# A weight decoder's sign words: read from the scaled word in SBUF instead of the raw word, in a fused attention and two-layer expert kernel

## The chip, the cores and the metric

The kernel runs on one core of a Trainium2 chip. The metric is device microseconds of one execution, lower is better; the time of a kernel is the median of its runs.

## The reference

Windowed attention with four sink positions is followed by two expert layers, each on the output of the one before. The inputs are float32 values that were multiplied by 8 and come to the kernel as float64.

```python
# attention: 2 batches, 8 heads, 768 positions, head size 64
scores = np.where(is_sink | in_window, scale * q @ k.T, -1e9)   # window 128, 4 sinks
a = exp(scores - max); a = a / (a.sum() + 1e-9); x = a @ v      # -> (1536, 512)
# first layer, 512 -> 2048 -> 512
h = np.maximum(x @ w_in, 0.0)
x = h * h @ w_out
# second layer, 512 -> 2048 -> 512
h = x @ w_in
P = a[0] + a[1] * h + a[2] * h**2 + a[3] * h**3
Q = 1.0 + abs(b[0]) * abs(h) + abs(b[1]) * h**2
return (P / (Q + 1e-6)) @ w_out
```

## The kernel before

**Weights.** Each layer's hidden size of 2048 is cut into 16 chunks of 128. A chunk holds the 512 x 128 piece of `w_in` and the 128 x 512 piece of `w_out` as 128 partitions x 1024 columns, so there are 32 chunks. `load_chunk` brings one in as two halves of 512 columns, here called a pair of halves; there are 64 halves. Each half comes by one DMA of 512 KB (L56, queue of SP) as two 32-bit words for each weight, the low and the high word of the float64, into a raw tile `wr` (three buffers). ScalarE scales the high word as if it were a float32 (L63, into `wt`), and writes the sign of the high word as a 16-bit value into the upper half of each word of a sign tile (L65; two sign tiles are used in turn). VectorE shifts the low word and puts the sign into it (L66, in place in `wr`), then shifts `wt` and puts that in (L67, in place in `wt`). The float32 weight stands in `wt` then; ScalarE casts it to the matmul type (L299, tile `wh`) and GpSimd takes the rest (L300, tile `wl`). `wt` has two buffers, and one comes free with L300 of its half. The raw tile comes free with its last reader, L67.

**Matmuls.** Every product is made of three: high x high, low x high, high x low. A unit is one chunk on one group of tokens: `gemm1` makes h (L400, 12 matmuls), an activation follows, its result is split into gh and gl (L407 ScalarE, L409 GpSimd), and `gemm2` adds to four accumulators (L439 in the first layer, L441 in the second, 12 matmuls). A unit of 512 tokens is 24 matmuls. The activation of the first layer is a relu (L128, ScalarE) and a product (L130, VectorE); that of the second is a rational function: L159, L161, L163, L168, L169 on ScalarE, L164 on GpSimd, L165, L166, L170, L171, L172 on VectorE.

**Stages.** Each layer works through its chunks in three stages of 6, 5 and 5. In a stage, all groups of tokens pass its chunks; then the accumulators are added to a sum in SBUF by VectorE (L465 in the later stages). The first stage of the first layer has six groups of 256 tokens and runs among the attention's blocks, each named by batch, pair of 256 positions and pair of heads, as e_1_2; the later stages have three groups of 512. Seven slots (`WSLOTS`) hold chunks, and four more are there from the second stage on, when the attention's pools are closed. A chunk is loaded into the slot of one whose last group has passed.

**Order.** The work is written in the order of the units, and a scheduler that knows the operations' dependencies turns it into a fixed order for each engine. An instruction waits for its semaphores, and all behind it on its engine wait too. The four L465 of a group stand in VectorE's order among the L66 and L67 of halves that are loaded meanwhile, and the first matmuls of the next group's accumulators can't start until these L465 have read the old ones. In the attention, the row maxima and masked scores come from VectorE (L341), and matmuls of the scores (L329) need the buffers that these free.

Of the kernel before, what the change touches and what calls it, by code (L numbers as in the profile page):

```python
# [10 lines left out]
F16 = mybir.dt.float16  # L11
# [29 lines left out]
def f32(ap):  # L41
    return ap.bitcast(F32)
# [10 lines left out]
def narrowed(nc, pool, src, n, signs):  # L53

    raw = pool.tile([P, 512, 2], U32, tag="wr", name=f"wr{n}", bufs=3)
    nc.sync.dma_start(raw.rearrange("p c w -> p (c w)"), src.bitcast(U32))  # L56
    lo, hi = raw[:, :, 0], raw[:, :, 1]
    t = pool.tile([P, 512], U32, tag="wt", name=f"wt{n}")
    s = signs[0]
    signs.append(signs.pop(0))  # L60


    nc.scalar.mul(f32(t), f32(hi), 2.0**-112)  # L63

    nc.scalar.mul(s.bitcast(F16).rearrange("p (c w) -> p c w", w=2)[:, :, 1], f32(hi), 2.0**-112)  # L65
    nc.vector.scalar_tensor_tensor(out=lo, in0=lo, scalar=29, in1=s, op0=ALU.logical_shift_right, op1=ALU.bitwise_or)  # L66
    nc.vector.scalar_tensor_tensor(out=t, in0=t, scalar=3, in1=lo, op0=ALU.logical_shift_left, op1=ALU.bitwise_or)  # L67
    return f32(t)
# [107 lines left out]
def banded(ctx, tc, const, qk0, qk1, vb, vs, ns_f, win_f, wp, ab, scalars, out):  # L176
# [115 lines left out]
    def load_chunk(L, pool=wpool):  # L292
        home[L] = pool
        h = pool.tile([P, 1024], F32R, tag="wh", name=f"wh{L}")
        lo = pool.tile([P, 1024], F32R, tag="wl", name=f"wl{L}")
        for i in range(2):
            c = slice(i * 512, (i + 1) * 512)
            t = narrowed(nc, wraw, wp[L][:, c], f"{L}_{i}", signs)
            nc.scalar.copy(h[:, c], t)  # L299
            nc.gpsimd.tensor_tensor(out=lo[:, c], in0=t, in1=f32(h[:, c]), op=ALU.subtract)  # L300
        wh[L], wl[L] = h, lo
# [271 lines left out]
def dense(tc, qk0, qk1, vb, ns_f, win_f, wp, ab, out):  # L573
# [75 lines left out]
    with xT_ctx, ExitStack() as ctx:  # L649
        wk = ctx.enter_context(tc.tile_pool(name="d_f", bufs=2))  # L650
        ps_a = ctx.enter_context(tc.tile_pool(name="d_pa", bufs=4, space=PSUM))
        ps_h = ctx.enter_context(tc.tile_pool(name="d_ph", bufs=2, space=PSUM))
        for ph in range(2):
            X = yT if ph else xT
            for g in range(NT // 512):
                cols = slice(g * 512, (g + 1) * 512)
                acc = [ps_a.tile([P, 512], F32, tag="acc", name="d_acc") for _ in range(4)]
                for f in range(NF):
                    wi = narrowed(nc, wk, wp[ph * NF + f][:, 0:512], f"d{ph}{g}{f}i", signs)
                    wo = narrowed(nc, wk, wp[ph * NF + f][:, 512:1024], f"d{ph}{g}{f}o", signs)  # L660
                    h = ps_h.tile([P, 512], F32, tag="h", name="d_h")
                    for k in range(4):
                        nc.tensor.matmul(h, lhsT=wi[:, k * P : (k + 1) * P], rhs=X[:, k, cols], start=k == 0, stop=k == 3)
                    y = rational(nc, wk, h, ab, con) if ph else squared_relu(nc, wk, h)
                    for m in range(4):
                        blk = slice(m * P, (m + 1) * P)
                        l, r = (y[:, blk], wo) if ph else (wo[:, blk], y)
                        nc.tensor.matmul(acc[m], lhsT=l, rhs=r, start=f == 0, stop=f == NF - 1)
                for m in range(4):
                    if ph == 0:  # L670
                        nc.vector.tensor_copy(yT[:, m, cols], acc[m])
                    else:
                        o = wk.tile([P, 512], F32, tag="o", name="d_out")
                        nc.scalar.mul(o, acc[m], -1.0)
                        t0 = g * 512 + m * P
                        nc.sync.dma_start(out[t0 : t0 + P, :], o)
# [58 lines left out]
```

## Time and profile before

| | |
|---|---|
| median of 3 runs | 687.01 us (686.88 to 688.39) |
| the profiled execution | 685.88 us, of which the profile's span is 684.2 us |
| mean granted clock of TensorE, share of full speed | 0.99 |
| busy in the span | TensorE matmul 95%, VectorE 68%, ScalarE 67%, GpSimd 59% |
| DMA of weights | 64 transfers of 512 KB |

The profiled execution takes 1.7 us more than its span, and 1.13 us less than the median. Busy shares are means over stages that differ. Times in the rows are microseconds from the start of the span; the engines are PE (TensorE matmul), PEld (its weight load), DVE (VectorE), ACT (ScalarE), POOL (GpSimd) and SP (SyncE).

### The profile page before, as it was taken

The page shows a single profiled execution, that of the slowest core. Times are in us where ns is not written, and L with a number is a line of the kernel's source. Part 1 is how long each engine was busy: PE and PEld are TensorE (multiplying, and loading weights), DVE is VectorE, ACT ScalarE, POOL GpSimd, SP SyncE. Part 2 cuts the span into 40 slices and gives each one's busy share as a digit, 9 for nine tenths or more (in the row PEclk, how much of TensorE's full clock was granted, in tenths as well). Part 3 has the DMA queues.
Part 4 walks back from the last instruction along what each step waited for, and adds up shares of the span by engine and source line. Part 5 has one row for each costly group of instructions (what it writes and reads, how often), then busy time and mean ns, then how long its engine had stood idle before and what let it go on. Part 6 is the DMA issues. An engine that isn't in the chain of part 4 may idle for free.

```text
span 684.2 us, 10131 instructions
## 1 busy us (share of the span) xinstructions
PE 648.0 (95%) x3376; PEld 528.2 (77%) x3376; DVE 467.9 (68%) x969; ACT 460.1 (67%) x938; POOL 401.5 (59%) x367
## 2 busy tenths in 40 slices
PE   4799999999999997999999998899998999999995
PEld 2456779999999875888778886688887888888884
DVE  7878855879842897427631279976699777577674
ACT  6767755777654876427542489886899866766761
POOL 4757855788753776327454579654577644544441
PEclk9999999999999999899999999999999999999998
DMA  7546632354200645204500033200030000001011
GB/s 249 186 134 184 204 90 69 103 135 131 67 25 1 210 160 182 65 1 137 171 0 1 0 124 103 82 1 1 1 123 32 0 1 1 0 1 61 3 61 68
DMA packets 25725, 54.16 MB, mean 79 GB/s; under 512 B 2880, under 2 KB 11072, under 8 KB 25664
## 3 DMA queue, kind: packets, MB, share of 16 engines
q1 hardware_dynamic: 25664, 53.43, 24.5%
q8 instruction: 29, 0.48, 0.3%
q14 instruction: 32, 0.26, 0.1%
HBM read 50.27 MB, written 3.15 MB: 78 GB/s over the span
## 4 chain that ended last, share of the span: by engine, by line
PE 63%; DVE 16%; ACT 8%; DMA 7%; issue 3%; POOL 2%; DVEq 0%; POOLq 0%; ACTq 0%
PE h L400 27%; PE acc L441 14%; PE acc L439 13%; DMA wr<-in_wp 6%; DVE wt L67 5%; DVE wr L66 4%; PE xo L382 3%; ACT sign L65 2%; PE pt L357 1%; PE s L329 1%; ACT wh L299 1%; ACT wt L63 1%; PE xo L385 1%; PE s L332 1%; POOL wl L300 1%
## 5 line engine op out<-in xcount | busy, mean ns | idle before, releaser
L409 POOL TENSOR_TENSOR gl<-sq,gh 128x256 fp32r<-128x256 f32 (+1 forms) x66 | 72.0, 1093 | 80.3 <-ACT gh L407 45.8
L164 POOL TENSOR_TENSOR z<-z,u 128x512 f32<-128x512 f32 x48 | 63.6, 1326 | 84.8 <-ACT z L163 81.5
L300 POOL TENSOR_TENSOR wl<-wt,wh 128x512 fp32r<-128x512 f32 x64 | 91.4, 1439 | 19.9 <-ACT wh L299 19.9
L66 DVE SCALAR_TENSOR_TENSOR wr<-wr,sign 128x512 uint32<-128x512 uint32 x64 | 64.2, 1003 | 19.6 <-ACT sign L65 19.5
L409 POOL TENSOR_TENSOR gl<-z,gh 128x512 fp32r<-128x512 f32 x47 | 62.1, 1322 | 24.8 <-ACT gh L407 21.2
L67 DVE SCALAR_TENSOR_TENSOR wt<-wt,wr 128x512 uint32<-128x512 uint32 x64 | 68.4, 1069 | 10.9 <-ACT wt L63 10.3
L130 DVE TENSOR_TENSOR sq<-sq,h 128x256 f32<-128x256 f32 (+1 forms) x66 | 35.5, 538 | 58.9 <-ACT sq L128 58.1
L439 PE MATMUL acc<-gh,wh 128*128 128x256 f32 (+1 forms) x264 | 66.2, 339 | 5.6 <-ACT sq L128 4.1
L65 ACT ACTIVATE sign<-wr 128x512 f16<-128x512 f32 x64 | 50.6, 790 | 24.6 <-DMA wr<-in_wp 24.4
L439 PE MATMUL acc<-gl,wh 128*128 128x256 f32 (+1 forms) x264 | 64.9, 336 | 0.5 <-POOL gl L409 0.5
L439 PE MATMUL acc<-gh,wl 128*128 128x256 f32 (+1 forms) x264 | 64.7, 334 | 0.0
L170 DVE SCALAR_TENSOR_TENSOR z<-z,con,h 128x512 f32<-128x512 f32 x48 | 35.8, 745 | 41.6 <-ACT h L169 40.1
L400 PE MATMUL h<-xh,wh 128*128 128x256 f32 (+1 forms) x264 | 61.6, 347 | 0.5 <-DVE sq L130 0.5
L128 ACT ACTIVATE sq<-h 128x256 f32<-128x256 f32 (+1 forms) x66 | 31.5, 477 | 45.3 <-PE h L400 34.5
L441 PE MATMUL acc<-wh,gh 128*128 128x512 f32 x192 | 60.2, 393 | 1.2 <-ACT gh L407 1.2
L441 PE MATMUL acc<-wl,gh 128*128 128x512 f32 x192 | 59.6, 390 | 0.0
L400 PE MATMUL h<-x2h,wh 128*128 128x512 f32 x192 | 53.9, 398 | 4.6 <-DVE z L172 4.6
L400 PE MATMUL h<-xl,wh 128*128 128x256 f32 (+1 forms) x264 | 58.2, 337 | 0.0
L400 PE MATMUL h<-xh,wl 128*128 128x256 f32 (+1 forms) x264 | 58.2, 338 | 0.0
L441 PE MATMUL acc<-wh,gl 128*128 128x512 f32 x192 | 57.6, 389 | 0.0
L439 PEld LDWEIGHTS acc<-gh,wh 128*128 128x128 f32 x264 | 44.5, 192 | 13.4 <-ACT wh L299 4.8
L352 POOL TENSOR_TENSOR e<-e,rs 128x320 f32<-128x320 f32 x48 | 37.2, 778 | 28.0 <-DVE rs L350 20.4
(104 smaller groups left out, 1591.9 us busy)
## 6 DMA issues: line engine op xcount, KB each, us to landing
wr<-in_wp SPq DMA_DIRECT2D x64, 512.0 KB, 3.7
qkr<-in_qk SPq DMA_DIRECT2D x32, 176.0 KB, 3.1
v<-in_vb SPq DMA_DIRECT2D x16, 192.0 KB, 2.7
out<-accsb SPq DMA_DIRECT2D x12, 256.0 KB, 2.1
qkr<-in_qk SPq DMA_DIRECT2D x8, 352.0 KB, 3.5
qkr<-in_qk SPq DMA_DIRECT2D x16, 136.0 KB, 2.8
qkr<-in_qk SPq DMA_DIRECT2D x4, 272.0 KB, 5.0
v<-in_vb SPq DMA_DIRECT2D x8, 128.0 KB, 3.6
```

Source lines behind the costliest of these rows:

```text
L65: nc.scalar.mul(s.bitcast(F16).rearrange("p (c w) -> p c w", w=2)[:, :, 1], f32(hi), 2.0**-112)
L66: nc.vector.scalar_tensor_tensor(out=lo, in0=lo, scalar=29, in1=s, op0=ALU.logical_shift_right, op1=ALU.bitwise_or)
L67: nc.vector.scalar_tensor_tensor(out=t, in0=t, scalar=3, in1=lo, op0=ALU.logical_shift_left, op1=ALU.bitwise_or)
L130: nc.vector.tensor_tensor(out=r, in0=r, in1=h, op=ALU.mult)
L164: nc.gpsimd.tensor_tensor(out=z, in0=z, in1=u, op=ALU.mult)
L170: nc.vector.scalar_tensor_tensor(out=z, in0=z, scalar=con[:, 2:3], in1=h, op0=ALU.add, op1=ALU.mult)
L300: nc.gpsimd.tensor_tensor(out=lo[:, c], in0=t, in1=f32(h[:, c]), op=ALU.subtract)
L352: nc.gpsimd.tensor_tensor(out=eq, in0=eq, in1=rs[:, c].unsqueeze(2).to_broadcast([P, 2, W]), op=ALU.mult)
L400: nc.tensor.matmul(h[:, :n], lhsT=w_[:, k * P : (k + 1) * P], rhs=x_[:, k, c0 : c0 + n], start=p_ + k == 0, stop=p_ + k == 5)
L409: eng.tensor_tensor(out=gl[:, :n], in0=y, in1=f32(gh[:, :n]), op=ALU.subtract)
L439: nc.tensor.matmul(acc[m][:, :n], lhsT=w_[:, 512 + m * P : 512 + (m + 1) * P], rhs=g_[:, :n], start=st, stop=sp, skip_group_check=True)
L441: nc.tensor.matmul(acc[m], lhsT=g_[:, m * P : (m + 1) * P], rhs=w_[:, 512:1024], start=st, stop=sp)
```

## The change

L65 reads the scaled word of `wt` that L63 has just written, with the factor 1, where it read the raw high word (every second word of `wr`) with the factor 2^-112. The value written is the same.

```diff
     nc.scalar.mul(f32(t), f32(hi), 2.0**-112)
 
-    nc.scalar.mul(s.bitcast(F16).rearrange("p (c w) -> p c w", w=2)[:, :, 1], f32(hi), 2.0**-112)
+    nc.scalar.mul(s.bitcast(F16).rearrange("p (c w) -> p c w", w=2)[:, :, 1], f32(t), 1.0)
     nc.vector.scalar_tensor_tensor(out=lo, in0=lo, scalar=29, in1=s, op0=ALU.logical_shift_right, op1=ALU.bitwise_or)
     nc.vector.scalar_tensor_tensor(out=t, in0=t, scalar=3, in1=lo, op0=ALU.logical_shift_left, op1=ALU.bitwise_or)
```

L65 now depends on L63, and the two DVE operations behind it come no earlier than a free buffer of `wt`. The scheduler then gives other orders on all engines. In the pieces that follow, a name's last number is a running number of the tile, and 0 or 1 before it is the half.

On ACT, in the second stage of the first layer, while its first group passes, it was before:

```order
L65 ACTIVATE sign_93<-wr_0_3292 128x512
L299 CAST wh_3270<-wt_1_3283 128x512
L407 CAST gh<-sq 128x512
L65 ACTIVATE sign_94<-wr_1_3301 128x512
L63 ACTIVATE wt_0_3294<-wr_0_3292 128x512
L65 ACTIVATE sign_93<-wr_0_3312 128x512
L63 ACTIVATE wt_1_3303<-wr_1_3301 128x512
L128 ACTIVATE sq<-h 128x512
L299 CAST wh_3290<-wt_0_3294 128x512
L299 CAST wh_3290<-wt_1_3303 128x512
```

and now it is:

```order
L63 ACTIVATE wt_0_3274<-wr_0_3272 128x512
L65 ACTIVATE sign_93<-wt_0_3274 128x512
L407 CAST gh<-sq 128x512
L63 ACTIVATE wt_1_3283<-wr_1_3281 128x512
L65 ACTIVATE sign_94<-wt_1_3283 128x512
L299 CAST wh_3270<-wt_0_3274 128x512
L128 ACTIVATE sq<-h 128x512
L299 CAST wh_3270<-wt_1_3283 128x512
L63 ACTIVATE wt_0_3294<-wr_0_3292 128x512
L65 ACTIVATE sign_93<-wt_0_3294 128x512
```

Before, the L65 of a half could stand ahead of the L63 of an earlier half (L65 of 3312 ahead of L63 of 3303); now each stands behind the L63 of its own half, in 26 of the 64 halves directly.

On DVE, at the end of that first group (the sum accsb_0 is that of group 0), it was before:

```order
L67 SCALAR_TENSOR_TENSOR wt_0_3334<-wt_0_3334,wr_0_3332 128x512
L66 SCALAR_TENSOR_TENSOR wr_1_3341<-wr_1_3341,sign_94 128x512
L67 SCALAR_TENSOR_TENSOR wt_1_3343<-wt_1_3343,wr_1_3341 128x512
L66 SCALAR_TENSOR_TENSOR wr_0_3790<-wr_0_3790,sign_93 128x512
L465 TENSOR_TENSOR accsb_0_1191<-accsb_0_1191,acc 128x512
L130 TENSOR_TENSOR sq<-sq,h 128x512
L465 TENSOR_TENSOR accsb_0_1191<-accsb_0_1191,acc 128x512
```

and now it is:

```order
L66 SCALAR_TENSOR_TENSOR wr_1_3301<-wr_1_3301,sign_94 128x512
L67 SCALAR_TENSOR_TENSOR wt_1_3303<-wt_1_3303,wr_1_3301 128x512
L465 TENSOR_TENSOR accsb_0_1191<-accsb_0_1191,acc 128x512
L130 TENSOR_TENSOR sq<-sq,h 128x512
L465 TENSOR_TENSOR accsb_0_1191<-accsb_0_1191,acc 128x512 x2
L66 SCALAR_TENSOR_TENSOR wr_0_3312<-wr_0_3312,sign_93 128x512
L465 TENSOR_TENSOR accsb_0_1191<-accsb_0_1191,acc 128x512
```

The first L465 stood behind L67 of the half 3343 and L66 of the half 3790; it stands behind L67 of the half 3303 now, which is four L67 and five L66 earlier.

On DVE in the attention of the second batch, at the block e_1_2, it was before:

```order
L66 SCALAR_TENSOR_TENSOR wr_1_583<-wr_1_583,sign_94 128x512
L341 ISA e_1_1_479,nm_1_1_476<-s_1_1_11_495,add_117 128x160
L341 ISA nm_1_1_476 128x1
L67 SCALAR_TENSOR_TENSOR wt_0_576<-wt_0_576,wr_0_574 128x512
L349 TENSOR_SCALAR rs_1_1_478<-sm_1_1_477 128x2
```

and now it is:

```order
L66 SCALAR_TENSOR_TENSOR wr_0_554<-wr_0_554,sign_93 128x512
L341 ISA e_1_1_479,nm_1_1_476<-s_1_1_11_495,add_117 128x160
L341 ISA nm_1_1_476 128x1
L349 TENSOR_SCALAR rs_1_1_478<-sm_1_1_477 128x2
L67 SCALAR_TENSOR_TENSOR wt_0_556<-wt_0_556,wr_0_554 128x512
```

At the same place in the attention the weights have come less far. Counted over all rows of DVE, the L66 and L67 ahead of the first L341 of a block go from 19 to 14 at e_1_2, from 25 to 18 at e_1_3 and from 27 to 24 at e_2_0.

## Rows read from the trace of the kernel before

**Rows 1.** The page: busy time of each engine.
```profile
PE 648.0 (95%) x3376; PEld 528.2 (77%) x3376; DVE 467.9 (68%) x969; ACT 460.1 (67%) x938; POOL 401.5 (59%) x367
```

**Rows 2.** Stretch, length, busy of PE, PEld, DVE, ACT, POOL, clock, DMA share, GB/s.
```profile
0.00:80.00 80.00, 63.14 (x286) 39.83 (x287) 65.54 (x219) 57.42 (x158) 53.53 (x61) 1.00 0.60 194
220.00:282.00 62.00, 57.38 (x269) 46.82 (x268) 48.86 (x56) 45.26 (x80) 41.27 (x30) 0.94 0.51 170
395.00:440.00 45.00, 40.98 (x176) 32.43 (x175) 41.35 (x53) 40.93 (x70) 35.81 (x25) 1.00 0.34 117
490.00:530.00 40.00, 38.23 (x166) 30.77 (x165) 35.89 (x46) 37.58 (x65) 29.68 (x22) 1.00 0.20 66
```

**Rows 3.** TensorE's waits: total us, times, longest.
```profile
PE s L329 <- DVE nm L341: 6.8, 6, 3.0
PE h L400 <- DVE z L172: 4.6, 3, 2.3
PE acc L439 <- ACT sq L128: 4.1, 1, 4.1
PE acc L439 <- ACT gh L407: 1.5, 1, 1.5
```

**Rows 4.** Timeline of TensorE: start, duration, instruction, idle time before and releaser.
```profile
238.89 1.10 PE L400 MATMUL h<-xh,wh 128*128 128x512 f32 x4
...
267.85 0.63 PE L400 MATMUL h<-xh,wh 128*128 128x512 f32 x2
272.53 0.76 PE L439 MATMUL acc<-gh,wh 128*128 128x512 f32 x1 [4.05 <-ACT sq L128]
```

**Rows 5.** Timeline of DVE and then ACT around 270 us.
```profile
270.47 0.69 DVE L67 SCALAR_TENSOR_TENSOR wt<-wt,wr 128x512 uint32<-128x512 uint32 x1
271.10 0.69 DVE L66 SCALAR_TENSOR_TENSOR wr<-wr,sign 128x512 uint32<-128x512 uint32 x1
271.70 0.68 DVE L465 TENSOR_TENSOR accsb<-accsb,acc 128x512 f32<-128x512 f32 x1
...
270.29 0.78 ACT L65 ACTIVATE sign<-wr 128x512 f16<-128x512 f32 x1 [1.43 <-DMA wr<-in_wp]
```

**Rows 6.** Busy time by stretches behind that stall.
```profile
270.00:275.00 5.00, 2.47 (x6) 2.02 (x7) 4.01 (x7) 3.52 (x7) 2.56 (x2) 0.55 0.59 202
275.00:280.00 5.00, 5.00 (x18) 3.92 (x18) 4.36 (x7) 2.36 (x6) 1.35 (x1) 0.76 0.42 122
```

**Rows 7.** Timeline of ACT, the first pair of the stretch; then GpSimd, third pair.
```profile
220.14 0.67 ACT L63 ACTIVATE wt<-wr 128x512 f32<-128x512 f32 x1
...
235.36 1.30 POOL L300 TENSOR_TENSOR wl<-wt,wh 128x512 fp32r<-128x512 f32 x1 [1.28 <-ACT wh L299]
```

**Rows 8.** Groups by line on ACT: busy us, mean ns, idle before and releasers.
```profile
L65 ACT ACTIVATE sign<-wr 128x512 f16<-128x512 f32 x64 | 50.6, 790 | 24.6 <-DMA wr<-in_wp 24.4
L63 ACT ACTIVATE wt<-wr 128x512 f32<-128x512 f32 x64 | 42.3, 663 | 4.4 <-POOL wl L300 4.2
L299 ACT CAST wh<-wt 128x512 fp32r<-128x512 f32 x64 | 38.9, 617 | 11.5 <-DVE wt L67 11.4
```

**Rows 9.** By line: ns min/median/max, first and last start in us.
```profile
L66 DVE SCALAR_TENSOR_TENSOR wr<-wr,sign x64: 678/694/1811, 11.1 to 519.9; 128x512 uint32<-128x512 uint32 x64
L67 DVE SCALAR_TENSOR_TENSOR wt<-wt,wr x64: 666/1060/1828, 12.0 to 525.6; 128x512 uint32<-128x512 uint32 x64
L300 POOL TENSOR_TENSOR wl<-wt,wh x64: 1264/1306/1773, 14.9 to 529.5; 128x512 fp32r<-128x512 f32 x64
```

**Rows 10.** Timeline of ACT: two dependent neighbours, and two casts of different halves.
```profile
484.66 0.72 ACT L168 ACTIVATE u<-z,con 128x512 f32<-128x512 f32 x1 [0.48 <-POOL z L164]
485.42 0.69 ACT L169 ACTIVATE h<-u,con 128x512 f32<-128x512 f32 x1
...
490.88 1.12 ACT L299 CAST wh<-wt 128x512 fp32r<-128x512 f32 x2
```

**Rows 11.** Timeline of ACT at 341 us.
```profile
341.31 0.77 ACT L65 ACTIVATE sign<-wr 128x512 f16<-128x512 f32 x1 [2.59 <-DMA wr<-in_wp]
```

## The prediction

> **What bounds the kernel now.** I read the busy shares first: TensorE's matmuls fill 95% of the span, VectorE and ScalarE two thirds [rows 1]. So a microsecond of ScalarE is worth nothing by itself; time can be won or lost only where TensorE idles. The windows show where that is [rows 2]. In the first 80 us, with the attention, it idles 80 - 63.14 = 16.9 us; in 220 to 282 us, the second stage's first group, 62 - 57.38 = 4.6; in 395 to 440, 45 - 40.98 = 4.0; in 490 to 530, 40 - 38.23 = 1.8. In the two late stretches ScalarE (40.93 of 45, 37.58 of 40) and VectorE (41.35 of 45, 35.89 of 40) are full as well, in the other two they have room. TensorE's waits then name what it waited for [rows 3]: row maxima of the attention on VectorE (L341, 6.8 us in 6 waits), the last operation of the rational function (L172, 4.6 us in 3), one single stall of 4.1 us at L439, and one of 1.5 us for gh (L407).
>
> The stall of 4.1 us is the one to follow. It lies between 268.48 (267.85 + 0.63) and 272.53 us [rows 4]. The releaser that the row names, the relu, is not it: the order shows that the first matmul of a new group needs the old accumulators read by L465, and the first L465 ran at 271.70, straight behind an L66 at 271.10, which had to have the L65 that ran from 270.29, after 1.43 us of waiting for the DMA of its raw words [rows 5]. So TensorE waited for a transfer of weights that it did not need at that time. Behind it the granted clock was 0.55 for 5 us and 0.76 for 5 more [rows 6], so 2.47 x 0.45 + 5.00 x 0.24 = 2.3 us went to a lower clock.
>
> **The change, part by part.**
>
> *The operation itself.* L65 is 790 ns in the mean [rows 8]. It reads every second word and writes every second 16-bit value. L63 reads every second word and writes whole words, 663; L299 reads and writes whole words, 617. So the stride of what is read is worth about 46 ns, and 64 x 0.046 = 2.9 us of ScalarE at most. ScalarE is full only in the late stretches, with 15 of these halves or fewer in each (15 x 0.046 = 0.7 us); I take 0.
>
> *The new neighbour.* L65 waits for the L63 just ahead of it in 26 of 64 halves. Dependent neighbours start 0.76 us apart where the first lasts 0.72 [rows 10], so there is no overlap; two casts of different halves take 1.12 us, 0.11 less than 2 x 0.617. So a dependent pair costs about 0.14 us more, 26 x 0.14 = 3.6 us of ScalarE, nearly all of it where ScalarE has room. The Trainium skill, "ScalarE: Activation LUTs", section "What ACT_TABLE_LOAD costs", says that neighbouring ACTIVATEs overlap by about 93 ns; the trace agrees roughly, with 0.11, and by the page the loss would be 26 x 0.093 = 2.4 us. In the full stretches I charge 1 us for it.
>
> *The stall at 268 us* (-6.9). Before, nine pairs of halves (chunks 3068 to 3330) ran from L63 at 220.14 to the end of L67 at 270.47 + 0.69 = 271.16: 51.0 / 9 = 5.67 us a pair [rows 5, 7]. In the new order the first L465 stands behind the seventh pair instead of behind the ninth and an L66. Is a pair longer now? With two buffers of wt, one half's chain L63, L65, L66, L67, L299, L300 sets the cycle of a pair. By medians it is 0.66 + 0.79 + 0.69 + 1.06 + 0.62 + 1.31 = 5.13 us; with the three longest of L66, L67 and L300 it is 0.66 + 0.79 + 1.81 + 1.83 + 0.62 + 1.77 = 7.48; with the shortest, 0.66 + 0.79 + 0.68 + 0.67 + 0.62 + 1.26 = 4.68 [rows 8, 9]. I take 5.7, the pace measured before, which lies between. Then the seventh pair is done at 220.14 + 7 x 5.7 = 260.0, and L465 waits only for TensorE's last matmul of its own accumulator. The stall would come back if 220.14 + 7c + 0.68 passed 268.48, that is from c = 6.8 us. Chunk 3172, the third pair, needs the same look: its low part was ready at 235.36 + 1.30 [rows 7], and its matmuls began at 238.89 [rows 4]. The new order puts 12 matmuls of 0.23 us (40.98 / 176, [rows 2]) ahead of them, so its low part, four matmuls in, is needed at 238.89 + 2.8 + 0.9 = 242.6; it comes at 220.14 + 3c + 1.3, 238.5 at c = 5.7, and is late from c = 7.0. So the stretch should give back its 4.6 us of idle time and the 2.3 of the clock, 6.9. Bounds: -6.9 and 0 (at the longest chain, 7.48, the two lateness terms are 220.14 + 22.4 + 1.3 - 242.6 = 1.3 and 220.14 + 52.4 + 0.68 - 268.48 = 4.7 in all, the idle time of before).
>
> *The wait for gh* (-1.5). The 1.5 us [rows 3] came because L407 stood on ScalarE behind an L65 that waited 2.59 us for its DMA until 341.31 [rows 11]. In the new order L65 follows its own L63, and L407 stands behind other instructions. I take the whole 1.5; the other bound is 0, if the L63 there waits as L65 did.
>
> *The attention* (-2). With weights behind by 5 to 7 instructions of L66 and L67 at the blocks of the second batch, VectorE comes to the row maxima earlier, by 5 x 1.0 to 7 x 1.07 (means, near the medians 0.69 and 1.06, [rows 9]), so 3.5 to 7 us. But it is busy 65.54 of 80 us [rows 2], the same halves must still be done before the stage's units need them, and only the waits for L341, 6.8 us, can shrink. I take -2, nearer to nothing than to the whole; bounds -6 and +3, the latter if the last three pairs of the stage are late by three halves of about 1 us each.
>
> *The late stretches* (+1). Up to three halves' L65 and L66 ran ahead of their L63 at each change of stage, in time that was idle. Now they stand in the full stretches: 3 x 0.79 = 2.4 us on ScalarE, 3 x 0.69 to 3 x 1.81, so 2 to 5 us, on VectorE [rows 8, 9]. Against that stands a lighter load ahead of the L172 that TensorE waits for (12 of L66 and L67 instead of 15 ahead of the fifth of them). I take these as even, and +1 for the dependent neighbours; bounds -4 and +6 for both stretches.
>
> **Sum.** -6.9 - 1.5 - 2 + 1 = -9.4. Some of what is won will be found again as a shorter wait elsewhere; one more microsecond for new waits on the two wt buffers, as L63's present 4.2 us for L300 show that these are not always free [rows 8]. That makes about -8: the profiled execution's 685.88 becomes 677.9. It was 1.13 below the median of the runs, so the forecast is 679.0. Less than 0.2%, 1.4 us, cannot be told from no change here.
>
> **The rivals.**
>
> *The two wt buffers become the bound (slower).* Each half now holds its wt through L65, too, and L66 can't run ahead. For it speaks that L66 and L67 have maxima of 1.8 us beside medians of 0.69 and 1.06, and that L63 waits for L300 already. If GpSimd's L300 stands beside most of them, c is 7.48: the stretch at 220 gives nothing, and the two full stretches lose what moves into them, 3 us each, with 0.56 us of clock for each us of idle time (2.3 / 4.05), so 6 x 1.56 = 9.4; less 1.5 and 2 that are still won: +6, about 693. It decides from c = 6.8 to 7.0 us. Against it: it wants all of L66 and L67 at their slow form, and medians say that half are fast. The Trainium skill, "SBUF — State Buffer", section "SBUF: two separate sides", says that a VectorE operation with two inputs in SBUF and a GpSimd one that reads SBUF exclude each other for a whole instruction. The spread of L66, 678 to 1811, agrees with that rule in kind. Chance 0.2, with other ways to be slower.
>
> *The stall moves (same).* The 6.9 are won, and come back where ScalarE and VectorE are full: 490 to 530 has 2.4 us of ScalarE's idle time left, and the three moved halves want 2.4, with VectorE's up to 5 beside it. A loss of 3 in each and its clock, 9.4, less 9.4 won is 0: 686 to 688. Chance 0.15.
>
> *It is hidden (same).* If L465 still waits for other work on VectorE, all that changes is ScalarE's 2.9 us against 3.6, off the path: 687. Its chance is within the last one.
>
> *The attention gives all.* If the waits for L341 shrink by 6 instead of 2 and the late stretches cost nothing, the sum is -6.9 - 1.5 - 6 = -14.4: 672.6. Chance 0.12.
>
> *My forecast*, 674 to 683: 0.53.
>
> **Range and chances.** Faster by over 0.2%: 0.53 + 0.12 = 0.65; within: 0.15; slower: 0.2. The range goes from 672.6 to 690: it leaves out some of the slower rival and a little below. The forecast's own range is 674 to 683.
>
> **What would show it.** In the changed profile: no wait of TensorE over 1 us between 260 and 280 us, and a granted clock near 1 there; L465 straight behind its matmuls; pairs of L63 under 6.8 us apart after 220; no wait of 1.5 us for L407; L65 near 745 ns; waits for L341 at 4 to 5 us in all; waits for L172 still about 4.6. It is wrong if pairs come 7 us apart, if L63's wait for L300 has grown to tens of us and TensorE's waits name weights (L299, L300), or if L172's waits have grown by over 5 us.

## The result, and the profile after

The changed kernel takes 661.73 us in the median of 4 runs (658.01 to 666.26), where the kernel before takes 686.94 (684.94 to 688.39): a ratio of 0.9638, 95% interval 0.9573 to 0.9703. It is faster by 25 us. The forecast was 679.0, with 672.6 as the lower end. Its four executions spread over 8 us, and the shorter ones have the higher mean granted clock (658.01 us at 0.995, 666.26 at 0.985). The profiled execution takes 661.41 us, with a span of 659.7 against 684.2.

(One correction to the text ahead of the prediction, which the prediction shares: a block's name as e_1_2 leaves out its batch in those rows, and e_1_2, e_1_3 and e_2_0 are blocks of the first batch, not of the second. The L341 in the rows shown there belongs to e_1_1, the block ahead of e_1_2.)

The page's first part of the changed kernel, which answers to [rows 1]:

```profile
PE 638.3 (97%) x3376; PEld 523.5 (79%) x3376; DVE 464.2 (70%) x969; ACT 459.9 (70%) x938; POOL 400.1 (61%) x367
```

The same matmuls keep TensorE busy 9.7 us less, and its idle time falls from 684.2 - 648.0 = 36.2 to 659.7 - 638.3 = 21.4 us. VectorE and ScalarE have as much work as before. TensorE's waits in the changed kernel (total us, times, longest) answer to [rows 3]:

```profile
PE s L329 <- DVE nm L341: 2.5, 2, 1.9
PE h L400 <- DVE z L172: 2.1, 3, 1.1
PE acc L439 <- ACT wh L299: 1.2, 1, 1.2
```

The row maxima cost 2.5 us in place of 6.8, L172 2.1 in place of 4.6, the stall of 4.1 is one of 1.2, and the wait of 1.5 for gh is gone. The groups on ScalarE (busy us, mean ns, idle before) answer to [rows 8]:

```profile
L65 ACT ACTIVATE sign<-wt 128x512 f16<-128x512 f32 x64 | 50.5, 789 | 0.8
L63 ACT ACTIVATE wt<-wr 128x512 f32<-128x512 f32 x64 | 42.8, 668 | 5.7 <-POOL wl L300 5.6
L299 ACT CAST wh<-wt 128x512 fp32r<-128x512 f32 x64 | 39.3, 620 | 28.0 <-DVE wt L67 27.0
```

This is the row to see. L65 itself is as long as before, 789 ns; but ScalarE stood 24.4 us in 23 waits ahead of L65 for the transfer of raw words, and now waits for no raw word at all, at L63 either. Part of the waiting has moved: ahead of L299 it stands 27.0 us for L67 on VectorE now, where it stood 11.4.

**Where the 24.5 us of the spans lie.** One place can be found in every version of the kernel: the first of the matmuls that end the first group of the second stage. Up to there TensorE has done the same work. The windows from the start to that place, in the kernel before and in the changed kernel (columns as in [rows 2]):

```profile
0.00:261.47 261.47, 244.59 (x1648) 202.83 (x1649) 193.46 (x583) 178.69 (x482) 177.03 (x201) 0.99 0.43 130
```

```profile
0.00:248.07 248.07, 237.73 (x1648) 199.31 (x1649) 185.92 (x578) 174.10 (x475) 171.69 (x198) 0.99 0.42 130
```

So 261.47 - 248.07 = 13.4 us are won by that place: 16.88 - 10.34 = 6.5 of idle time, and 244.59 - 237.73 = 6.9 because the same 1648 matmuls took less time. Behind it come 0.54 + 4.05 - 1.23 = 3.4 of the stall, the 2.3 of the lower clock that followed it, 1.5 at gh, 4.6 - 2.1 = 2.5 at L172 and 1.2 at gh in the second layer (1.2 us in the waits of before, none after): 24.3 in all.

The 6.9 us I put down to TensorE's clock. One matmul of each block, L385, shows the change, in the timeline of the kernel before and then of the changed one (start, duration):

```profile
50.00 0.58 PE L385 MATMUL xo<-sT,vsh 128*128 128x256 f32 x1
57.23 0.39 PE L385 MATMUL xo<-sT,vsh 128*128 128x256 f32 x1
```

```profile
19.78 0.58 PE L385 MATMUL xo<-sT,vsh 128*128 128x256 f32 x1
27.93 0.39 PE L385 MATMUL xo<-sT,vsh 128*128 128x256 f32 x1
39.24 0.58 PE L385 MATMUL xo<-sT,vsh 128*128 128x256 f32 x1
49.06 0.39 PE L385 MATMUL xo<-sT,vsh 128*128 128x256 f32 x1
```

Before, it takes 0.58 us in every block up to 50 us and 0.39 from 57 us on; after, it is short from 28 us on, but for one block at 39 us, after idle pieces around 35 us. The window around that block in the changed kernel has a granted clock of 0.50:

```profile
38.00:44.00 6.00, 6.00 (x25) 4.38 (x24) 3.85 (x13) 4.08 (x12) 2.91 (x5) 0.50 0.42 156
```

So the long ones are at the lower of the two levels, 1.2 GHz, and the short ones at 2.4. The granted clock in [rows 2] is 1.00 for the first 80 us of the kernel before, and does not show this: the first clock record of its trace is at 52.1 us (27.5 in the changed kernel), and the windows count the time ahead of it as 1.00. In the changed kernel TensorE is busy in all of 20 to 30 us, where it was busy 8.3 of 10 before, and there the matmuls become short. The Trainium skill, "TensorE: Matmul & The Clock Gate", section "What's actually happening", says that a gate lets half or all of the clock's pulses through to the array and that activity opens it; the trace agrees in kind, 0.58 us at a granted clock of 0.50 against 0.39 at 1.00.

**When the start's gain is made.** The L385 at 50.00 us before and the one at 39.24 us after belong to the same block, the fourth. So 10.8 us are won by then, with 123 matmuls done before and 119 after. (At the next blocks the lead is 7 to 14 us, since the units of the first stage stand between the blocks at other places.) Up to there TensorE waited 6.0 us for row maxima before and 1.9 after. ScalarE had not yet waited for raw words in either profile; its first such wait in the kernel before ends at 55.48 us:

```profile
55.48 0.79 ACT L65 ACTIVATE sign<-wr 128x512 f16<-128x512 f32 x1 [2.18 <-DMA wr<-in_wp]
```

TensorE's longest wait for a row maximum is at the third block. In the kernel before, VectorE and then TensorE; and VectorE in the changed kernel:

```profile
13.51 0.86 DVE L66 SCALAR_TENSOR_TENSOR wr<-wr,sign 128x512 uint32<-128x512 uint32 x1
14.40 1.09 DVE L67 SCALAR_TENSOR_TENSOR wt<-wt,wr 128x512 uint32<-128x512 uint32 x1
15.42 1.76 DVE L66 SCALAR_TENSOR_TENSOR wr<-wr,sign 128x512 uint32<-128x512 uint32 x1
...
18.23 0.31 DVE L341 CUSTOM_DVE_ANT_0 e<-s,add 128x160 f32<-128x160 f32 x1
...
18.61 1.57 PE L329 MATMUL s<-qkr 64*128 64x288 f32 x4 [3.03 <-DVE nm L341]
```

```profile
13.87 0.69 DVE L66 SCALAR_TENSOR_TENSOR wr<-wr,sign 128x512 uint32<-128x512 uint32 x1
14.48 0.32 DVE L341 CUSTOM_DVE_ANT_0 e<-s,add 128x160 f32<-128x160 f32 x1
```

Counted from the start, five L66 and L67 stand ahead of the first row maximum of the third block before, and three after.

### The profile page after: what moved, and what is told of

Same layout as the page of the kernel before. It is cut to its first block, busy times and chain, and to the rows that moved or that the text cites. A ratio compares the mean times of both kernels' runs of the same rounds, so it can differ in the third digit from the quotient of the medians.

```text
span 659.7 us, 10180 instructions
## 1 busy us (share of the span) xinstructions
PE 638.3 (97%) x3376; PEld 523.5 (79%) x3376; DVE 464.2 (70%) x969; ACT 459.9 (70%) x938; POOL 400.1 (61%) x367
## 4 chain that ended last, share of the span: by engine, by line
PE 72%; DVE 13%; ACT 7%; issue 3%; POOL 2%; DMA 1%; SPq 0%; DVEq 0%; ACTq 0%; POOLq 0%
PE h L400 31%; PE acc L441 16%; PE acc L439 15%; DVE wt L67 4%; PE xo L382 3%; DVE wr L66 3%; ACT sign L65 2%; PE s L329 2%; PE pt L357 2%; ACT wt L63 1%; POOL wl L300 1%; PE xo L385 1%; PE s L332 1%; DVE h L171 1%; PE s L331 1%
## 5 line engine op out<-in xcount | busy, mean ns | idle before, releaser
L300 POOL TENSOR_TENSOR wl<-wt,wh 128x512 fp32r<-128x512 f32 x64 | 91.2, 1433 | 28.5 <-ACT wh L299 26.0
L409 POOL TENSOR_TENSOR gl<-sq,gh 128x256 fp32r<-128x256 f32 (+1 forms) x66 | 69.6, 1055 | 63.1 <-ACT gh L407 26.9
L409 POOL TENSOR_TENSOR gl<-z,gh 128x512 fp32r<-128x512 f32 x47 | 63.8, 1358 | 30.4 <-ACT gh L407 22.4
L66 DVE SCALAR_TENSOR_TENSOR wr<-wr,sign 128x512 uint32<-128x512 uint32 x64 | 60.3, 942 | 26.7 <-ACT sign L65 26.5
L67 DVE SCALAR_TENSOR_TENSOR wt<-wt,wr 128x512 uint32<-128x512 uint32 x64 | 67.4, 1053 | 3.6
L439 PE MATMUL acc<-gh,wh 128*128 128x256 f32 (+1 forms) x264 | 65.0, 334 | 1.2 <-ACT wh L299 1.2
L439 PE MATMUL acc<-gh,wl 128*128 128x256 f32 (+1 forms) x264 | 64.1, 332 | 0.0
L439 PE MATMUL acc<-gl,wh 128*128 128x256 f32 (+1 forms) x264 | 64.1, 335 | 0.0
L299 ACT CAST wh<-wt 128x512 fp32r<-128x512 f32 x64 | 39.3, 620 | 28.0 <-DVE wt L67 27.0
L400 PE MATMUL h<-x2l,wh 128*128 128x512 f32 x192 | 53.6, 396 | 0.0
L400 PE MATMUL h<-x2h,wl 128*128 128x512 f32 x192 | 53.2, 396 | 0.0
```

Of the source, the lines that this page charges most:

```text
L400: nc.tensor.matmul(h[:, :n], lhsT=w_[:, k * P : (k + 1) * P], rhs=x_[:, k, c0 : c0 + n], start=p_ + k == 0, stop=p_ + k == 5)
L409: eng.tensor_tensor(out=gl[:, :n], in0=y, in1=f32(gh[:, :n]), op=ALU.subtract)
L439: nc.tensor.matmul(acc[m][:, :n], lhsT=w_[:, 512 + m * P : 512 + (m + 1) * P], rhs=g_[:, :n], start=st, stop=sp, skip_group_check=True)
```

## The experiments

All times stand against runs of the kernel before on the same chip, whose medians were 686.6 to 687.6 us. "Place" is the time of the place named above on TensorE; "raw waits" is the time that ScalarE stood waiting for raw words at L63 and L65, in the profile.

| kernel | median us | ratio to before (95%) | place | raw waits |
|---|---|---|---|---|
| before | 686.94 | 1 | 261.47 | 24.4 |
| changed | 661.73 | 0.957 to 0.970 | 248.07 | 0 |
| first_seven | 675.10 | 0.976 to 0.986 | 249.22 | 22.3 |
| all_but_first_seven | 669.88 | 0.969 to 0.977 | 256.05 | 3.9 |
| raw_source_tied | 680.06 | 0.985 to 0.994 | 254.13 | 14.3 |
| filled_start | 687.88 | 0.999 to 1.005 | 260.23 | 22.3 |
| order_only | 665.77 | 0.966 to 0.973 | 250.50 | 0 |
| order_vector_only | 683.79 | 0.993 to 0.997 | 259.29 | 21.3 |
| two_raw_buffers | 677.09 | 0.983 to 0.993 | 253.54 | 31.8 |
| three_wt_buffers | 679.81 | 0.987 to 0.994 | 252.74 | 32.3 |
| sums_early | 681.20 | 0.990 to 0.996 | 261.37 | 20.5 |
| changed_sums_early | 661.91 | 0.956 to 0.966 | 249.76 | 0 |
| changed_two_raw | 671.75 | 0.971 to 0.980 | 253.30 | 23.8 |
| weights_back_start | 682.31 | 0.992 to 0.996 | 257.23 | 25.5 |
| changed_later | 662.90 | 0.962 to 0.970 | 251.83 | 0 |

before_again, run once, took 687.93 us. In the short diffs, `after(a, b)` tells the scheduler that `a` stands behind `b` on the engine that both run on; it adds no wait, and `L` is the chunk.

**The change in halves.** first_seven has the new L65 for the first seven chunks, all_but_first_seven for the rest.

```diff
-    nc.scalar.mul(s..., f32(hi), 2.0**-112)
+    new = L < 7            # all_but_first_seven: L >= 7
+    nc.scalar.mul(s..., f32(t) if new else f32(hi), 1.0 if new else 2.0**-112)
```

> L65 reads wt for the 14 halves of the first seven chunks (those loaded among the attention) and the raw word for all others; the rows of VectorE ahead of the attention's blocks are then those of the changed kernel up to e_2_1, and the first L465 stands where it stood before. Theory A (the gain at the start comes from the order of the first 14 halves against the attention): 10 to 15 us faster than before, the sums of the first group at 85 to 89 us, and the stall at L439 of about 4 us at the end of the second stage's first group still there. Rival B (the gain at the start is luck of that execution, or comes from later halves): within 2 us of before.

> The complement: L65 reads the raw word for the first seven chunks and wt for the other 25. Theory A: 9 to 13 us faster, the sums of the first group still near 99 us, no stall of 4 us at the first L465, and no wait of 1.5 us for gh. The two halves of the change should add up to the whole, about 25 us, within 4. Rival B (start and rest work on each other): their sum differs from the whole by over 6 us.

The first gained 13 us by its ratio, took 12 off the start (place at 249.22) and kept the stall, 5.3 us there, as theory A has it. The second gained 18, more than the 9 to 13 expected: its stall is 1.7 us and the wait for gh is gone, but the first group's sums came at 94 us, not near 99, and its place came 5.4 us earlier too, with the idle time hardly changed (256.05 - 239.44 = 16.6) and matmuls that took 5.2 us less. By the place the halves are not independent: they win 12.3 + 5.4 = 17.7 us there, where the whole change wins 13.4. The two gains in time sum to 31 against 25; with intervals of 7 and 5 us wide the excess of 6 doesn't decide rival B.

**Is it the word that is read?** order_only keeps the raw word and only tells the scheduler that L65 comes behind its own L63 on ScalarE. raw_source_tied keeps it too, and ties the sign tile to L300 of two halves before.

```diff
# order_only
+    i63 = nc.scalar.mul(f32(t), f32(hi), 2.0**-112)
+    i65 = nc.scalar.mul(s..., f32(hi), 2.0**-112)
+    after(i65, i63)        # order on the engine alone, no wait
# raw_source_tied, behind L300
+            nc.gpsimd.tensor_scalar(out=signs[-1].bitcast(F16)[:, 0:1], in0=f32(lo[:, i * 512 : i * 512 + 1]), scalar1=0.0, scalar2=0.0, op0=ALU.mult, op1=ALU.add)
```

> The kernel before (L65 reads the raw word), with one rule for the scheduler: on ScalarE, L65 of a half stands behind L63 of the same half. No wait is added, since both are on ScalarE. Theory A (what matters is that L65 no longer stands ahead of its time in ScalarE's order): as the changed kernel, 658 to 668 us; the first group's end in the second stage at 247 to 252 us on TensorE (248.07 in the changed kernel, 261.47 before); ScalarE's waits for raw words at L65 fall from 24 us to under 5. Rival C (reading the scaled word, contiguous and in SBUF already, is what gains): 680 us or more.

> L65 reads the raw word as before, but after L300 GpSimd writes a zero into the sign tile's low half word (it is zero already), from a word of the wl that L300 made. So an L65 waits for the L300 of two halves before, as L63 does through wt, without reading what L63 wrote. It adds 64 GpSimd operations on 128 x 1. Theory A (only the hold on running ahead matters, not the word that is read): the first L465 stands as far ahead as in the changed kernel, the attention's blocks are half way between (17 of L66 and L67 ahead of e_1_2, where 19 and 14 stand in the two kernels); 10 to 20 us faster than before. Rival C (reading the scaled word is what gains): within 3 us of before.

order_only gains 21 of the 25 us with the raw word read as ever; its L65 takes 783 ns. That refutes rival C. The rule names ScalarE alone, but the scheduler gave VectorE another order with it: 4 of L66 and L67 ahead of the third block, 10, 12, 16, 20, 24 ahead of e_1_0 to e_2_0, and 60 ahead of the first L465. The window up to its place:

```profile
0.00:250.50 250.50, 235.90 (x1649) 198.20 (x1650) 182.33 (x579) 175.09 (x477) 173.05 (x199) 1.00 0.43 131
```

It has more idle time than the changed kernel (14.6 us) and shorter matmuls (235.90). raw_source_tied gained 7 us, less than expected: its L65 still waited 14.3 us for raw words and 9.7 more for L66. It is below the 10 to 20 us of theory A and above the 3 of rival C. The tie sets no place behind L63; that this is why it gained less was not shown.

**VectorE's order or ScalarE's waits.** Four kernels with the raw word, each with one edit, in turn: L66 behind the L67 of the half before; two raw tiles in place of three; the four L465 of group 0 ahead of L66 of the chunk 3290; L66 of six early halves behind the row maxima of a block of the attention.

```diff
# order_vector_only
+    i66 = nc.vector.scalar_tensor_tensor(out=lo, ...)
+    after(i66, last_i67)
# two_raw_buffers
-    raw = pool.tile([P, 512, 2], U32, tag="wr", name=f"wr{n}", bufs=3)
+    raw = pool.tile([P, 512, 2], U32, tag="wr", name=f"wr{n}", bufs=2)
# sums_early
+                if (ph, sc, g, m) == (0, 1, 0, 3):
+                    after(i66["13_0"], ad)          # ad: this L465
# weights_back_start
+    after(i66[half], first_L341[block])   # 2_1: 0_1_0, 3_0: 0_1_1, 3_1: 0_1_2, 4_1: 0_1_3, 6_0: 0_2_0, 6_1: 0_2_1
```

> The kernel before, with another rule alone: on VectorE, L66 of a half stands behind L67 of the half before. L65 may still stand ahead on ScalarE, by the two sign tiles. Theory H (an L65 that stands early waits for its transfer, and holds up ScalarE's attention and activations behind it): ScalarE's waits for raw words stay above 12 us and the time within 5 us of before. Rival V (the harm was L66 in the way on VectorE): 678 us or less.

> The kernel before with two raw tiles in place of three, so that L65 can run ahead by one half less, and each transfer starts later. On VectorE 61 instead of 69 of L66 and L67 stand ahead of the first L465 (60 in the changed kernel), and 10, 14, 18, 22, 26 ahead of the blocks e_1_0 to e_2_0 (13, 16, 19, 25, 27 before; 10, 12, 14, 18, 24 in the changed kernel). Theory V (VectorE's order): half of the gain or more, 674 us or less. Theory H: L65 still stands ahead of its time and waits for later transfers; ScalarE's waits for raw words grow over 24 us, and the time is 680 us or more.

> The kernel before (L65 reads the raw word) with one rule: on VectorE, the four L465 of group 0 in the second stage stand ahead of L66 of the chunk 3290. So 55 instead of 69 of L66 and L67 stand ahead of the first L465. Theory V (the stall at 268 us was only the place of L465): the stall of 4.05 us goes, the clock stays up behind it, and the time falls by 5 to 8 us; the waits of L65 for raw words stay, and with them the start and the wait for gh. Rival H2 (the wait moves to another instruction behind an L65 on ScalarE): TensorE loses 3 us or more within the next 15 us, and the time falls by 3 us or less.

> The kernel before (L65 reads the raw word, and no rule for it), with rules on VectorE for six of the first 14 halves: L66 of that half stands behind the first L341 of a block of the attention. So 10, 12, 16, 19, 24 of L66 and L67 stand ahead of the blocks e_1_0 to e_2_0 (13, 16, 19, 25, 27 before; 10, 12, 14, 18, 24 in the changed kernel). Nothing after the start is ruled. Theory V (VectorE's order sets the start): 8 to 13 us faster, the first group's end in the second stage at 249 to 254 us on TensorE. Theory H (ScalarE's L65, early, set it): 4 us faster at most, that end at 257 us or later.

order_vector_only gained 3.5 us, as theory H expected. sums_early gained 5 us: the stall and the lower clock behind it went, the start and the wait for gh stayed, and ScalarE still waited 20.5 us for raw words. So the place of L465 is worth 5 us, the lower end of what theory V says. weights_back_start moved the place to 257.23, 4.2 us of the 13.4, and gained 4.1 us (interval 2.5 to 5.8), at theory H's bound of 4; theory V's 8 to 13 did not come. But it does not bound what VectorE's order is worth. It ruled the blocks from e_1_0 on; 5 and 9 of L66 and L67 still stood ahead of the third and fourth block (3 and 7 in the changed kernel), and TensorE's wait of 3.0 us at the third stayed. Sorted by that block, all kernels fall into two groups: with 3 or 4 of L66 and L67 ahead of it the place is at 248.07 to 254.13, with 5 at 256.05 to 261.47. No kernel moved this order alone, so that it is the cause was not shown. two_raw_buffers fell between the two: raw waits grew to 31.8 us, as H says, and it still gained 8 us by its ratio, as much as its place came earlier, though ScalarE's waits for raw words in the first 110 us were longer than before (4.9 against 3.8 us). At the start L65 ran ahead less: 2, 3, 4, 5, 6 of them stood ahead of the exponentials of e_1_0 to e_2_0, where 3, 5, 6, 7, 8 stood before. Its stall of 4.0 us stayed.

**Putting the waits back.** Two kernels on top of the change: two raw tiles in place of three, without and with a third wt buffer.

```diff
# both, on the changed kernel
-    raw = pool.tile([P, 512, 2], U32, tag="wr", name=f"wr{n}", bufs=3)
+    raw = pool.tile([P, 512, 2], U32, tag="wr", name=f"wr{n}", bufs=2)
# three_wt_buffers also
-    t = pool.tile([P, 512], U32, tag="wt", name=f"wt{n}")
+    t = pool.tile([P, 512], U32, tag="wt", name=f"wt{n}", bufs=3)
```

> The changed kernel with three wt buffers in place of two, and two raw tiles in place of three, since SBUF has no room for both. Theory R (with the change, the wt buffers set the pace of a pair, 6.5 to 6.8 us in its trace): L63 no longer waits for L300 (5.6 us in the changed kernel), pairs follow each other 6.2 us apart or less, the last 1.2 us of the stall at the first L465 are gone, and the time is 0 to 4 us under the changed kernel's 661.7. Rival T (the raw words' transfer sets it): pairs as far apart or further, the time at or above the changed kernel's.

> The changed kernel with two raw tiles in place of three, wt still with two. It parts the kernel with three wt buffers and two raw tiles (679.8 us) into its two edits. Theory H (ScalarE is held up by an instruction that stands there before its raw words have landed): with two raw tiles a transfer starts only when L67 of two halves before has ended, so L63 waits for it: ScalarE's waits for raw words are 15 us or more and the time is 670 to 682 us. Rival R (it was the third wt buffer): within 4 us of the changed kernel, 658 to 666 us.

With two raw tiles ScalarE stands 23.8 us for raw words, and 8 to 10 of the 25 us are lost again (by the ratio and by the medians); rival R falls. With the third wt buffer L63 waits 32.3 us for its words, and 18 are lost, 8 more than with two raw tiles alone. Its pairs follow each other (260.93 - 210.88) / 7 = 7.15 us apart, further than the changed kernel's 6.80 (below), so theory R falls, and both signs of rival T came. A stall of 3.9 us at the first L439 of the next group is back. A third wt buffer beside three raw tiles was not run.

**The clock at the start, and once more.** filled_start adds four transposes of the identity ahead of L382 in the first nine blocks of the kernel before; before_again is that kernel unchanged.

```diff
+        if (bb * NJ + j) * HP + hp < 9:
+            for _ in range(4):
+                nc.tensor.matmul(xo[:, 256:384], lhsT=ident, rhs=ident, is_transpose=True, start=True, stop=True)
```

> The kernel before, with four transposes of the identity added on TensorE ahead of each of the first nine blocks' L382, into columns of the bank that nobody reads. They add 36 matmuls, about 36 x 0.21 = 7.6 us at the lower clock or 4.3 at the higher, where TensorE waits for the probabilities anyhow; the weights stand no further back than before. Theory D (at the start TensorE's matmuls run at the lower of their two clock levels until about 51 us before and until about 27 us in the changed kernel, because it idles in pieces, and this is a good part of the 13 us): the same matmuls (L385 0.58 us at the lower level, 0.39 at the higher) become short 10 us or more earlier than in the kernel before, and the time falls by 3 to 9 us. Rival E (VectorE's order alone sets the start, the clock costs nothing): the matmuls may become short earlier, but the time stays or grows by up to 5 us.

> The kernel before once more, for a second profile of it. If the level of TensorE's clock in the first 110 us differs from execution to execution, TensorE's busy time for the first 1648 matmuls (up to the first group's end in the second stage) is other than the 244.6 us of the first profile, by some us, at the same count; if it is fixed by the order, it is 243 to 246 us again. Its idle time there should be 16 to 18 us either way.

```profile
0.00:260.23 260.23, 241.31 (x1685) 202.49 (x1686) 191.69 (x583) 178.45 (x482) 178.67 (x201) 0.98 0.43 131
```

L385 was short already at 24 and at 40 us, long at 32 and 47. TensorE did 36 more matmuls (the count of the window takes in the one at its end) in 3.3 us less busy time than before; but it idled 18.9 us, 2 more than before, and the time did not fall, which is what rival E says. The test is mixed: more of the weights stood ahead of the later blocks as well (32 of L66 and L67 at e_2_0 in place of 27), against what was expected. The second execution of the kernel before came to 244.32 us of busy time and 261.47 us at the place, so between these two executions of one order the level at the start did not change.

**Further than the change.** changed_sums_early puts the rule of sums_early on the changed kernel; changed_later lets eight early halves' L66 stand two to four places further back.

```diff
# changed_later, on the changed kernel
+    after(i66[half], first_L341[block])   # 2_0: 0_1_0, 2_1: 0_1_1, 3_0: 0_1_2, 4_0: 0_1_3, 5_0: 0_2_0, 5_1: 0_2_1, 6_0: 0_2_2, 6_1: 0_2_3
```

> The changed kernel with the same rule: the four L465 stand one pair of halves earlier than in the changed kernel (54 instead of 60 of L66 and L67 ahead). Expected: the stall of 1.23 us that is left there goes, 0.5 to 2 us faster than the changed kernel's 661.7, which is within its spread. Rival: the later pairs, one place back, hold up chunks for the next stage, and the time is 663 us or more.

> The changed kernel with such rules: L66 of eight halves of the start stands two to four places further back, 8, 10, 12, 16, 20, 22, 24 of L66 and L67 ahead of the blocks e_1_0 to e_2_2 (10, 12, 14, 18, 24, 26, 29 in the changed kernel). Theory V, if the gain goes on: 2 to 6 us faster than the changed kernel's 661.7. Rival W (the weights come too late for the first stage's units then): TensorE waits for L299 or L300 in the first 110 us, and the time is 664 us or more.

Neither differs from the changed kernel by more than its spread. The first lost the rest of the stall (no wait there at all) and has 0.6 us at a later sum instead; the second came to its place 3.8 us later. No kernel was clearly faster than the changed one.

## Why the prediction was wrong

**What held.** That L65's own time would gain nothing on the path; that the stall of 4.05 us and its clock would mostly go (5.7 us of the forecast 6.9; sums_early measured 5 by itself); that gh's 1.5 us would go wholly. The dependent pair has no overlap, as forecast: L63 and L65 of one half start 0.71 us apart at 249 us in the changed trace, where L63 lasts 0.68, with ScalarE's busy time as before.

**The step that failed: the attention.** "I take -2, nearer to nothing than to the whole", with -6 as the bound; the start, up to the place, gave -13.4. The step held that "only the waits for L341, 6.8 us, can shrink". These did shrink, by 4.3 us (0.6 of it came back at L382), which is inside its bound. Outside it lay the matmuls of the start, which took 6.9 us less and which the step put at nothing, and another 6.5 - 4.3 = 2.2 us of idle time. The step also counted VectorE's order from e_1_2 on, where the longest wait for L341 was already past; 10.8 us were won by the fourth block. And it looked at VectorE alone: with one rule for ScalarE, L65 behind its own L63, 11.0 of the 13.4 us are won (order_only), though VectorE's order changed with it.

**ScalarE's waits for raw words.** The 24.4 us of [rows 8] invite the reading that the attention stood behind an L65 that waited for its words. For the start this does not hold: only 3.8 us of them lie in the first 110 us, and the first ends at 55.48 us, when most of the start's gain had been made. They bear on the stall and on gh, where the prediction used 1.43 and 2.59 us of them. Over all kernels, the four whose ScalarE never waits for raw words take 661.7 to 665.8 us, and all that have 14 us of it or more take 671.8 or more, with the new L65 or the old, and with two raw tiles or three. But the times do not follow the size of the waits: 32.3 us of them go with 679.8 us, 24.4 with 686.9. How the start's gain divides between VectorE's order at the first blocks, the 0.8 us of work of each L65 ahead of the attention on ScalarE, and the clock that followed, was not parted.

**The clock.** By the sum, half of the start's gain, 6.9 us, is matmuls at the higher level. The prediction priced the clock only behind the stall, by the granted clock, and put nothing for the start, where the window said 1.00. Durations of one matmul over time would have shown 50 us at the lower level. Whether the level won time or only followed from the order is open: in filled_start the matmuls took 3.3 us less and the time did not fall.

**The pair's pace was also off**, without harm. I took 5.7 us and set 6.8 as the point from which the stall comes back. In the changed kernel, the first and the seventh pair, and TensorE:

```profile
207.16 0.67 ACT L63 ACTIVATE wt<-wr 128x512 f32<-128x512 f32 x1
```

```profile
254.04 0.69 DVE L67 SCALAR_TENSOR_TENSOR wt<-wt,wr 128x512 uint32<-128x512 uint32 x1
254.65 0.68 DVE L465 TENSOR_TENSOR accsb<-accsb,acc 128x512 f32<-128x512 f32 x1
```

```profile
253.62 0.63 PE L400 MATMUL h<-xh,wh 128*128 128x512 f32 x2
255.48 0.48 PE L439 MATMUL acc<-gh,wh 128*128 128x512 f32 x1 [1.23 <-ACT wh L299]
```

(254.04 + 0.69 - 207.16) / 7 = 6.80 us, just at that point, and 1.23 us of the stall are left. With the changed kernel's own times the stall comes back from (253.62 + 0.63 - 0.68 - 207.16) / 7 = 6.63 us on, and 7 x 0.17 = 1.2 us is what is left. The slower rival's mechanism was there, then, but not its price: L66 and L67 took 942 and 1053 ns in the mean, no more than before, and L63's waits for L300 went from 4.2 to 5.6 us. The long form of L66 and L67 did not spread. The prediction set it beside the rule of the Trainium skill, "SBUF — State Buffer", section "SBUF: two separate sides", by which a VectorE operation with two inputs in SBUF and a GpSimd one that reads SBUF exclude each other; no run here parts that rule from others.

**The late stretches** were forecast to cost 1 us, and 3.7 were won there (L172 and gh in the second layer). all_but_first_seven has L172's 2.1 us and first_seven 4.7, so this belongs to the later chunks' L65; that its waits for raw words there (0.63, 0.65 and 0.47 us at 429, 439 and 503 us before) are the cause was only argued.

**Signs and sums.** Of the signs that the prediction named, L65 near 745 ns (789 measured), waits for L341 at 4 to 5 us (2.5) and waits for L172 still about 4.6 (2.1) did not come. In the attention's working, 5 x 1.0 to 7 x 1.07 is 5.0 to 7.5 us, not 3.5 to 7; the -2 did not hang on it.

## What to carry to other kernels

When a scheduler fixes each engine's order, an edit that adds a dependency can move work on all engines, and its gain can then be a matter of order. Here a dependency that looks like a loss gained 25 us, and one rule that put L65 behind its own L63 on ScalarE, with the old read, gained 21 of them. So compare the orders from the first instruction on and on every engine: most of the start's gain was made in the first 50 us, ahead of the blocks that the prediction counted. An instruction that can stand ahead of its data may cost those behind it, and more buffers can let it stand there: with two raw tiles, a third wt buffer made the changed kernel 8 us slower. And look at the clock of a stretch by the duration of one and the same matmul over time, too.

## What the runs showed that was not expected

Reading contiguous words instead of every second word did not shorten L65: 790 to 789 ns, and 783 with the old read in the new order. So the stride of the read cost L65 nothing that can be seen, and the prediction's 46 ns for it, taken from L63 and L299, did not apply; what makes those two differ, no run parts.

The granted clock in the windows can stand at 1.00 where matmuls take 0.58 us that take 0.39 at another time of the same run: this is so ahead of the first clock record. Behind it, at 38 to 44 us of the changed kernel, the column and the durations agree.
